# One decode block on one core: TensorE's last part placed 820 unreached instructions further on, and one load of down weights cut into 113 and 15 rows

## The chip, the cores and the metric

The kernel runs on one core of a Trainium2 chip. The metric is the time of one execution in microseconds, as the device measures it. Beside the plain timed runs there is one profiled execution, whose records the views show.

## What is computed

One decode step of a transformer block, for two batch rows and one new position: layer norm, attention over a cache of 8192 keys in 16 heads of width 256, and a bilinear gated feed-forward part, all in float32.

```python
B, Sq, D, H, Sk, Dh, F = 2, 1, 448, 16, 8192, 256, 1792
q = (layernorm(x) @ wq) as (B, H, 1, Dh)
p = softmax(einsum("bhqd,bhkd->bhqk", q, k_cache) * Dh ** -0.5)
h = x + (einsum("bhqk,bhkd->bhqd", p, v_cache) as (B, 1, H * Dh)) @ wo
n = layernorm(h)
out = h + ((n @ w_gate) * (n @ w_up)) @ w_down
```

## The kernel before

The caches make nearly all of the bytes. There are 32 pairs of head and batch row, called turns here. A turn's keys are 8192 x 256 floats, 8 MB, and lie in SBUF as 128 partitions of 64 keys each; its values lie the same way. Two key buffers take turns (`k0`, `k1`), the values have one buffer (`v`). In each turn VectorE multiplies the keys by the spread query and adds over the width (L436, L445, in a part of 16 keys and one of 48), takes the maximum (L458, L464), ScalarE makes the exponentials (L494), and TensorE mixes the values with them (L527, 32 matmuls) and gathers the four column groups (L619).

All loads but that of x are issued by SyncE, on one queue, in the order written from L261 to L292. Each load is a transfer of 128 rows, one row per partition. A load waits at SyncE until its buffer is free: keys of turn i + 1 for the maximum of turn i - 1, values of turn i for the mix of turn i - 1. After the last turn's keys and values come the weights, into buffers that the caches no longer need: the output projection `wo` and, after the last maximum, the gate weights `wg` and the up weights `wu` in three loads go to the key buffers; the down weights go to the value buffer, so they wait for the last mix, ("M", 31). They are cut into six loads by `DOWN = (4, 4, 2, 2, 1, 1)`, numbered 0 to 5; a unit is 448 columns of 128 rows (224 KB). Load 2 thus has 128 rows of 3584 bytes. TensorE waits for each of the six by its own semaphore (`wd0` to `wd5`) at the first matmul that reads it.

Each engine's instructions are recorded in a list (`Engine.do`, `roll`) and written out by `Engine.emit` (L81). A `roll` becomes a loop in the program. TensorE's list is: a short first part, a loop over the groups of the query projection (L386), a loop of 32 turns (L627, whose body also has the last turn's extra work behind branches), and the last part from L631 on: filler matmuls on data that nobody reads (`busy`, L534), the last head's output projection (L577), the second layer norm, gate and up projections (L715, L726), the product's transposes (L760), and the down projection in two forms (L779 for the chunks of loads 0 and 1, L805 for the rest), of which VectorE copies the result (L815) and SyncE stores it (L818).

`emit` also writes, at the start of each engine's list or behind the first `ahead` entries, a prefetch hint for a branch, a register `never` that holds 0, and a compare-and-branch on it. The hinted branch is a single instruction `aside` behind the engine's main part, which is never reached, since `never` is not below 0.

Of the kernel before, what the change touches and what calls it, by code (L numbers as in the profile page):

```python
# [8 lines left out]
B, D, H, SK, DH, F = 2, 448, 16, 8192, 256, 1792  # L9
EPS = 1e-5  # L10
P = 128
# [3 lines left out]
NQ = H * B  # L15
# [10 lines left out]
FH = FG[0] // 2  # L26
FF = [(n, g) for n in range(4) for g in range(4) if n < FG[g] // P]
DOWN = (4, 4, 2, 2, 1, 1)
NPART, OPEN_AFTER = 8, 9

LAYOUT = (
# [6 lines left out]
class Engine:  # L38
# [3 lines left out]
    def __init__(self, nc, engine, name, *apart):  # L42
        self.nc, self.e, self.apart = nc, engine, apart
        self.sems = [nc.alloc_semaphore(name=f"{name}{k}") for k in range(1 + len(apart))]
        self.items, self.ahead, self.gap = [], 0, None

    def sem_of(self, done):
        return self.sems[next((k + 1 for k, a in enumerate(self.apart) if done[0] in a), 0)]
# [32 lines left out]
    def emit(self, known):  # L81


        e, nc, seen = self.e, self.nc, {}
        if self.ahead is None:
            return self.emit_ops(self.items, known, seen)
        here, name = [e.engine], f"{e.engine.name}_"
        never = e.alloc_register(name + "never")
        self.emit_ops(self.items[: self.ahead], known, seen)
        hint = e.mark_branch_hint_location()  # L90
        e.reg_mov(never, 0)
        e.br_lt(never, 0, on_true=name + "aside", on_false=name + "main")
        with nc.body(name + "main", valid_engines=here):
            self.emit_ops(self.items[self.ahead : self.gap], known, seen)
            nc.br(name + "rest", engines=here)
        with nc.body(name + "aside", valid_engines=here):
            e.br_lt(never, 0, on_true=name + "aside", on_false=name + "rest").branch_hint(hint)
        nc.switch_bb(name + "rest")
        if self.gap is not None:
            self.emit_ops(self.items[self.gap :], known, seen)  # L100
# [53 lines left out]
def decode_block(nc, x, k_cache, v_cache, wq, wo, wg, wu, wd, out):  # L154
# [6 lines left out]
    def landing(name):  # L161
        return nc.alloc_semaphore(name=name)

    bank = [nc.alloc_psum_tensor(f"bank{i}", [P, 512], F32)[:] for i in range(8)]
    known = {}
    first_sem = landing("none")
    V, A, G, S, T = (
        Engine(nc, *engine)
        for engine in (
            (nc.vector, "dve"), (nc.scalar, "act", ("qsel", "qb"), ("q",)), (nc.gpsimd, "pool"),  # L170
            (nc.sync, "sp"), (nc.tensor, "pe", ("qp", "Q0"), ("heads",)),
        )
    )

    def load(line, dst, src, sem, name, *waits, n=16):
        line.do(lambda: line.e.dma_start(dst, src).then_inc(sem, 16), *waits)  # L176
        known[name] = sem, n
# [3 lines left out]
    v_flat = v_sb.rearrange("p j d -> p (j d)")  # L181
# [93 lines left out]
    at = 0  # L275
# [9 lines left out]
        load(S, wu_t[:, part], wu[:, part], landing(f"wu{k}"), ("wu", k))  # L285
    at = 0
    for k, n in enumerate(DOWN):
        load(
            S, v_flat[:, at * D : (at + n) * D], wd[:, at * D : (at + n) * D],
            landing(f"wd{k}"), ("wd", k), ("M", NQ - 1),  # L290
        )
        at += n  # L292


# [330 lines left out]
                )  # L625

    T.roll(0, NQ, 1, tensor_turn)  # L627

# [42 lines left out]
    for rows, c, to in LAYOUT:  # L673
        k = rows.stop - rows.start
# [100 lines left out]

    down_of = [k for k, n in enumerate(DOWN) for _ in range(n)]
    for k, (j, g) in enumerate(FF[:NPART]):
# [44 lines left out]
    engines = (S, A, G, V, T)  # L822
# [60 lines left out]
```

## Time and profile before

| | |
|---|---|
| plain runs, median of 3 | 1301.5 us (1301.0 to 1301.56) |
| the profiled execution | 1300.94 us |
| its span, first to last instruction | 1299.6 us |
| bytes read and written in HBM | 561.19 MB and 0.06 MB |
| VectorE busy | 1132.5 us (87%) |
| TensorE busy, matmuls | 471.1 us (36%) |
| mean granted TensorE clock | 0.64 of full speed |

The profile's page gives the time by engine and by line of the kernel; the DMA part gives packets, bytes and the share of the time of 16 DMA engines that the packets took. The chain of waits is followed back from the last instruction, at each step to what released it. The timeline lists instructions in order of time, with the idle time ahead of each and what ended it in square brackets. The windows give, for a stretch of time, its length, the busy time of the five engines (with the count of instructions), the granted TensorE clock, the mean share of the DMA engines that were busy (packets overlap, so that it can be above 1), and the GB/s moved.

### The profile page before, as it was taken

The numbers are of one execution on the slowest core, as the hardware profiler recorded it, in microseconds if no ns is written. First come the engines' busy times: TensorE is split into PE (matmuls) and PEld (weight loads), VectorE is DVE, ScalarE is ACT, GpSimd is POOL, SyncE is SP. The second block draws the span as 40 slices with busy tenths as digits, with TensorE's granted clock in tenths as the row PEclk, the third lists the DMA queues.
The fourth block names the chain that finished last, engine by engine and source line by source line (L and its number), as shares of the span: only waits on it lengthen the run. The fifth ranks groups of instructions, "written<-read, shape, count | busy, mean of one in ns | idle before, by whom it ended". The sixth has DMA issues, their size and how long they took to land.

```text
span 1299.6 us, 7381 instructions
## 1 busy us (share of the span) xinstructions
PE 471.1 (36%) x2870; PEld 149.9 (12%) x2870; DVE 1132.5 (87%) x265; ACT 83.5 (6%) x245; POOL 0.8 (0%) x8
## 2 busy tenths in 40 slices
PE   3643214334323433323334322433322343332368
PEld 0111001101001101101101101101100110100113
DVE  1999988889888889888889988889988888988861
ACT  1100000000000000000000000000000000000000
POOL 0000000000000000000000000000000000000000
PEclk9866566666566666556666656666656666655669
DMA  9999999999999999999999999999999999999998
GB/s 412 428 450 422 448 424 444 426 436 436 422 450 422 450 422 448 424 444 426 436 436 422 450 422 450 422 448 424 444 426 436 436 422 450 422 450 422 448 422 365
DMA packets 11382, 561.28 MB, mean 432 GB/s; under 512 B 1394, under 2 KB 1652, under 8 KB 2420
## 3 DMA queue, kind: packets, MB, share of 16 engines
q1 hardware_dynamic: 11376, 561.25, 99.8%
q8 instruction: 2, 0.03, 0.0%
q10 hardware_dynamic: 4, 0.00, 0.0%
HBM read 561.19 MB, written 0.06 MB: 432 GB/s over the span
## 4 chain that ended last, share of the span: by engine, by line
DMA 48%; DVE 41%; issue 8%; PE 2%; SPq 0%; DVEq 0%; ACT 0%
DMA k<-in_A_k_cache_dram 45%; DVE s L445 21%; DVE k L436 19%; DMA v<-in_wq_dram 2%; DMA v<-in_wd_dram 1%; PE bank L376 1%; PE bank L561 1%; PE bank L527 1%; DVE m L458 0%; DVE nm L464 0%; DVE rl L469 0%; SPq L176 0%; PE bank L551 0%; DVEq L149 0%; PE bank L367 0%
## 5 line engine op out<-in xcount | busy, mean ns | idle before, releaser
L436 DVE TENSOR_TENSOR k<-k,qb 128x4096 f32<-128x4096 f32 x64 | 555.3, 8676 | 122.6 <-DMA k<-in_A_k_cache_dram 98.9
L445 DVE TENSOR_REDUCE s<-k 128x16 f32<-128x4096 f32 x64 | 555.2, 8675 | 1.1
L527 PE MATMUL bank<-v,p 128*2 128x512 f32 x2048 | 289.5, 729 | 348.0 <-DMA v<-in_A_v_cache_dram 348.0
L527 PEld LDWEIGHTS bank<-v,p 128*2 128x2 f32 x2048 | 53.2, 96 | 577.2 <-DMA v<-in_A_v_cache_dram 370.7
L597 PE MATMUL bank<-nm,row 1*128 1x1 f32 x64 | 18.6, 357 | 230.9 <-DVE nm L464 230.9
L594 PE MATMUL bank<-ident,m 128*1 128x128 f32 x32 | 11.9, 372 | 179.7 <-DVE m L458 179.7
L502 ACT ACTIVATE o_sb<-bank 128x512 f32<-128x512 f32 x32 | 19.1, 597 | 625.9 <-PE bank L527 625.9
L597 PEld LDWEIGHTS bank<-nm,row 1*128 1x128 f32 x64 | 15.9, 306 | 240.3 <-DVE nm L464 240.3
L619 PE MATMUL bank<-sel,o_sb 128*128 128x1 f32 x256 | 33.7, 253 | 22.6 <-ACT o_sb L502 22.6
L367 PE MATMUL bank<-q_sel,ones 2*128 2x256 f32 x68 | 40.2, 691 | 0.0
L619 PEld LDWEIGHTS bank<-sel,o_sb 128*128 128x128 f32 x256 | 31.0, 191 | 52.3 <-ACT o_sb L502 52.3
L376 PE MATMUL bank<-v,xz 128*2 x64 | 30.5, 639 | 16.3 <-DMA v<-in_wq_dram 16.3
L492 ACT ACTIVATE nb<-bank 128x1 f32<-128x1 f32 x32 | 5.5, 171 | 427.0 <-PE bank L597 427.0
L601 PE MATMUL bank<-lsum,ones 128*128 128x1 f32 x64 | 18.7, 361 | 23.5 <-ACT p L494 23.5
L594 PEld LDWEIGHTS bank<-ident,m 128*1 128x1 f32 x32 | 2.5, 79 | 182.7 <-DVE m L458 182.7
L601 PEld LDWEIGHTS bank<-lsum,ones 128*128 128x128 f32 x64 | 16.0, 309 | 26.2 <-ACT p L494 26.2
L404 ACT ACTIVATE q_sel<-q_all,ident 2x256 f32 (+1 forms) x35 | 17.2, 492 | 0.0
L413 ACT ACTIVATE qb<-bank 128x256 f32<-128x256 f32 x34 | 13.0, 383 | 58.2 <-PE bank L367 58.2
L367 PEld LDWEIGHTS bank<-q_sel,ones 2*128 2x128 f32 x68 | 16.4, 297 | 2.2 <-issue 1.7
L494 ACT ACTIVATE p<-s,nb 128x64 f32<-128x64 f32 x32 | 11.1, 348 | 1.0
L504 ACT ACTIVATE oT<-bank,rl 128x2 f32 x32 | 8.4, 262 | 42.0 <-PE bank L619 42.0
L487 DVE COPY k<-bank 128x448 f32<-128x448 f32 x1 | 0.6, 624 | 11.6 <-PE bank L561 11.6
(89 smaller groups left out, 96.0 us busy)
## 6 DMA issues: line engine op xcount, KB each, us to landing
v<-in_wq_dram SPq DMA_DIRECT2D x1, 7168.0 KB, 19.7
k<-in_wo_dram SPq DMA_DIRECT2D x1, 7168.0 KB, 39.6
k<-in_A_k_cache_dram SPq DMA_DIRECT2D x1, 6144.0 KB, 38.1
v<-in_A_v_cache_dram SPq DMA_DIRECT2D x1, 6144.0 KB, 22.8
k<-in_wg_dram SPq DMA_DIRECT2D x1, 3136.0 KB, 27.8
k<-in_A_k_cache_dram SPq DMA_DIRECT2D x1, 2048.0 KB, 24.1
v<-in_A_v_cache_dram SPq DMA_DIRECT2D x1, 2048.0 KB, 27.3
k<-in_wu_dram SPq DMA_DIRECT2D x1, 1792.0 KB, 31.8
```

Source lines behind the costliest of these rows:

```text
L367: lambda *_: nc.tensor.matmul(qb_ps, ones[:B, :], q_sel, start=True, stop=True),
L376: lambda turn, k=k, c=c, xs=xs, base=base: nc.tensor.matmul(q_ps[k], xz[:, xs, :], wq_t[:, bass.ds(turn * QG + base, QG)], start=(c == 0), ...
L404: return nc.scalar.activation(q_sel, q_sb[:, bass.ds(at, DH)], AF.Copy, scale=ident[:B, b : b + 1])
L413: lambda *_: nc.scalar.activation(qb[i % 2], qb_ps, AF.Copy),
L436: lambda *_: nc.vector.tensor_mul(kt, kt, q[:, None, :].to_broadcast([P, hi - lo, DH])),
L445: lambda *_: nc.vector.tensor_reduce(s[:, lo:hi], kt, axis=AX.X, op=ALU.add),
L502: A.do(lambda *_: nc.scalar.activation(o_sb, o_ps, AF.Copy), ("M", i), done=("osb", i))
L527: lambda *_, t=t, g=g: nc.tensor.matmul(o_ps[g : g + 2, :], p_t[:, 2 * t : 2 * t + 2], v_sb[:, 2 * t : 2 * t + 2, :], start=(t < 4), stop= ...
L594: lambda *_: nc.tensor.transpose(mT_ps, m_t, ident), ("m", i), done=("T", i)
L597: lambda *_: nc.tensor.matmul(nb_ps, row, nm, start=True, stop=True),
L601: lambda *_: nc.tensor.matmul(l_ps, ones, lsum, start=True, stop=True),
L619: lambda *_, c=c, k=k: nc.tensor.matmul(oT_ps[:, c : c + 1], o_sb[:, (2 * k + c) * P : (2 * k + c + 1) * P], sel[:, k : k + 1], start=(k = ...
```

## The change

Two places change. First, TensorE's list gets a mark `far` behind the loop of turns. `emit` now writes the hint and the register at the start, all up to the mark, and then a compare-and-branch: if `never` is below 0 (it isn't) to a part `unused`, else to a part `far`. The hint at the start names this branch. `unused` is 1640 waits for a semaphore to be at least 0, which the built program holds as 820 instructions, and a branch; it lies between the loop and `far`, and is not reached. At `far` stand the hint, the register and the branch over `aside` that stood at the start before, and then the last part as it was. Second, load 2 of the down weights is issued as two transfers, of rows 0 to 112 and of rows 113 to 127, both to the semaphore `wd2`, whose wait asks for 32 in place of 16.

```diff
+APART, EVEN, ROWS = 820, 2, 113
...
-        self.items, self.ahead, self.gap = [], 0, None
+        self.items, self.ahead, self.gap, self.far, self.apart_by = [], 0, None, None, 0
...
         self.emit_ops(self.items[: self.ahead], known, seen)
+        at = self.ahead
+        if self.far is not None:
+            hint = e.mark_branch_hint_location()
+            e.reg_mov(never, 0)
+            self.emit_ops(self.items[at : self.far], known, seen)
+            e.br_lt(never, 0, on_true=name + "unused", on_false=name + "far").branch_hint(hint)
+            with nc.body(name + "unused", valid_engines=here):
+                for _ in range(2 * self.apart_by):
+                    e.wait_ge(self.sems[0], 0)
+                nc.br(name + "far", engines=here)
+            nc.switch_bb(name + "far")
+            at = self.far
         hint = e.mark_branch_hint_location()
         e.reg_mov(never, 0)
         e.br_lt(never, 0, on_true=name + "aside", on_false=name + "main")
         with nc.body(name + "main", valid_engines=here):
-            self.emit_ops(self.items[self.ahead : self.gap], known, seen)
+            self.emit_ops(self.items[at : self.gap], known, seen)
...
     for k, n in enumerate(DOWN):
-        load(
-            S, v_flat[:, at * D : (at + n) * D], wd[:, at * D : (at + n) * D],
-            landing(f"wd{k}"), ("wd", k), ("M", NQ - 1),
-        )
+        sem, parts = landing(f"wd{k}"), [slice(0, P)]
+        if k == EVEN:
+            parts = [slice(0, ROWS), slice(ROWS, P)]
+        for rows in parts:
+            load(
+                S, v_flat[rows, at * D : (at + n) * D], wd[rows, at * D : (at + n) * D],
+                sem, ("wd", k), ("M", NQ - 1), n=16 * len(parts),
+            )
         at += n
...
     T.roll(0, NQ, 1, tensor_turn)
+    T.far, T.apart_by = len(T.items), APART
```

On TensorE, where the loop of turns ends, the order was the following (`bank` is PSUM, `o_sb` the mixed values, `oT` the heads' results, `sel`, `heads` and `ident` constants or earlier results; the waits are for ScalarE's semaphore `act0`):

```order
L619 MATMUL bank<-sel,o_sb 128x1 [waits act0]
L619 MATMUL bank<-sel,o_sb 128x1 x3
L115 REGISTER_ALU
L115 COMPARE_AND_BRANCH
L539 MATMUL bank<-k,sel 2x256 x4
L581 MATMUL bank<-k,oT 2x256 [waits act0]
```

It now is this, with the line numbers of the changed file (L639 was L619, L559 was L539, L601 was L581; the 820 waits of `unused` are not listed, and lie ahead of the branch of L103):

```order
L639 MATMUL bank<-sel,o_sb 128x1 [waits act0]
L639 MATMUL bank<-sel,o_sb 128x1 x3
L131 REGISTER_ALU
L131 COMPARE_AND_BRANCH
L99 COMPARE_AND_BRANCH
L103 UNCONDITIONAL_BRANCH [waits pe0]
L106 BRANCH_PREFETCH_HINT
L108 COMPARE_AND_BRANCH
L559 MATMUL bank<-k,sel 2x256 x4
L601 MATMUL bank<-k,oT 2x256 [waits act0]
```

Behind the loop's own branch (L131) stands the new one (L99), which goes past L103 to L106; the matmuls and their waits are as before.

On SyncE, from the load of the up weights to the output, the order was the following (`k` and `v` are the buffers; the numbers are rows by floats):

```order
L176 DMA k<-in_wu_dram 128x896
L176 DMA v<-in_wd_dram 128x1792 [waits pe0]
L176 DMA v<-in_wd_dram 128x1792
L176 DMA v<-in_wd_dram 128x896 x2
L176 DMA v<-in_wd_dram 128x448 x2
```

It now is:

```order
L192 DMA k<-in_wu_dram 128x896
L192 DMA v<-in_wd_dram 128x1792 [waits pe0]
L192 DMA v<-in_wd_dram 128x1792
L192 DMA v<-in_wd_dram 113x896
L192 DMA v<-in_wd_dram 15x896
L192 DMA v<-in_wd_dram 128x896
L192 DMA v<-in_wd_dram 128x448 x2
```

One issue has become two, and loads 3 to 5 stand one issue later; nothing else on this queue is moved.

## The prediction

> **What bounds the kernel now.** I read the page's header and queue table first, then the end of the chain of waits, then the windows of the last microseconds. The page:
>
> ```profile
> span 1299.6 us, 7381 instructions
> ...
> DMA packets 11382, 561.28 MB, mean 432 GB/s; under 512 B 1394, under 2 KB 1652, under 8 KB 2420
> ...
> q1 hardware_dynamic: 11376, 561.25, 99.8%
> q8 instruction: 2, 0.03, 0.0%
> q10 hardware_dynamic: 4, 0.00, 0.0%
> ```
>
> SyncE's queue q1 keeps the 16 DMA engines busy for 99.8% of the span, so bytes per engine set the time. One engine moves 561.25 MB / (0.998 x 16 x 1299.6 us) = 27,046 bytes per us. The packet count also says how a transfer is dealt. The code issues 79 transfers of 128 rows on q1 (78 loads, one output), and 79 x (128 + 16) = 11,376: each row is a packet and each transfer has 16 more. These are the small ones: 79 x 16, 2 on q10 and the output's 128 rows of 448 bytes make the 1394 under 512 bytes. The last steps of the chain, with start, duration and what ran:
>
> ```profile
> 1278.38 0.42 SPq L176
> 1278.85 0.43 SPq L176
> 1279.31 17.89 DMA v<-in_wd_dram
> 1297.24 0.44 PE bank L805 x8
> 1297.71 0.27 DVE k L815
> ```
>
> The last load of down weights is issued by 1279.31 and lands about 1297.2, 17.89 us later, though it has 0.2 MB: it stands behind what is queued. From 1297.24 to the end of the span are 2.36 us. Windows (length, busy time of each engine, granted clock, mean DMA share, GB/s):
>
> ```profile
> 1290.00:1292.00 2.00, 2.00 (x16) 0.51 (x14) 0.74 (x2) 0.00 (x0) 0.00 (x0) 1.00 1.00 421
> ...
> 1295.00:1295.50 0.50, 0.35 (x16) 0.38 (x16) 0.50 (x1) 0.00 (x0) 0.00 (x0) 1.00 0.94 362
> 1295.50:1296.00 0.50, 0.50 (x20) 0.16 (x8) 0.06 (x1) 0.00 (x0) 0.00 (x0) 1.00 0.25 93
> 1296.00:1296.50 0.50, 0.36 (x18) 0.35 (x16) 0.00 (x0) 0.00 (x0) 0.00 (x0) 1.00 0.13 50
> 1296.50:1297.00 0.50, 0.50 (x20) 0.16 (x9) 0.00 (x0) 0.00 (x0) 0.00 (x0) 1.00 0.09 36
> 1297.00:1297.50 0.50, 0.34 (x12) 0.16 (x8) 0.00 (x0) 0.00 (x0) 0.00 (x0) 1.00 0.00 0
> ```
>
> The share falls from 0.94 to 0.25, then to 0.13 and 0.09: 0.13 x 16 is two engines. So some 14 engines are done near 1295.6 and about two work on until 1297.2. The kernel ends with its slowest DMA engine, some 1.6 us behind most. TensorE's timeline says how its last waits follow the loads:
>
> ```profile
> 1290.14 0.20 PEld L726 LDWEIGHTS bank<-k,xr 128*64 128x64 f32 x4 [0.84 <-DMA k<-in_wu_dram]
> ...
> 1293.93 0.93 PE L779 MATMUL bank<-v,k 128*2 128x448 f32 x8 [0.23 <-DMA v<-in_wd_dram]
> ...
> 1295.15 0.59 PE L805 MATMUL bank<-v,k 128*32 128x112 f32 x16 [0.29 <-DMA v<-in_wd_dram]
> ...
> 1296.15 0.93 PE L805 MATMUL bank<-v,k 128*32 128x112 f32 x24
> ...
> 1297.24 0.40 PE L805 MATMUL bank<-v,k 128*32 128x112 f32 x8 [0.16 <-DMA v<-in_wd_dram]
> ```
>
> From wu2 on TensorE waits for a load at nearly every group, but only 0.16 to 0.84 us each.
>
> **The load in two parts.** Load 2 of the down weights (448 KB, 128 rows of 3584 bytes, 8 rows per engine) becomes one of 113 and one of 15 rows. The bytes stay; what counts is which engine gets them. One more issue costs SyncE about 0.43 us (the chain's last SPq row), and it moves loads 3 to 5 back by that at the issue, about 17 us ahead of their landing; the output's issue waits for VectorE anyway. So that is nothing. Nothing waits earlier than before either: TensorE's wait for load 2 now asks for both parts. The deal is the whole cost. The trace shows one transfer with other than 128 rows, the two rows of x on ScalarE's queue, in the first 4 us:
>
> ```profile
> DMA packets 20, 0.92 MB, mean 230 GB/s; under 512 B 2, under 2 KB 4, under 8 KB 4
> ...
> q1 hardware_dynamic: 16, 0.92, 70.2%
> q10 hardware_dynamic: 4, 0.00, 0.6%
> ```
>
> Of q10's four packets two are rows (1792 bytes) and two are small: a transfer closes with one small packet for each engine that took part, two for two rows and 16 for 128. In both cases every engine had an equal share, 1 row or 8. By that, 15 rows go to 15 engines. But 113 is prime: equal shares exist only as 113 engines or as one, so one engine gets all 113. Unequal shares (8 rows on fourteen engines, 1 on a fifteenth, none on the last) are the other way; no row excludes them. I take equal shares, since nothing else occurs in the trace.
>
> [...]
>
> The sum. The one engine gets 113 rows and one of the 15, where it had 8: 106 more rows of 3584 bytes. At 27,046 bytes per us that is 106 x 0.1325 = 14.05 us. From the timeline: loads 4 and 5 (28,672 bytes per engine together) part the waits at 1296.15 and 1297.24, 1.09 us, so 0.136 us per 3584 bytes and 14.4 us in all. I take 14.2. Its queue then ends at 1295.6 + 14.2 = 1309.8, if it is one of the fourteen; loads 3 to 5 need their share of this engine too and land behind. The end moves from 1297.24 by 12.6 us. If it is one of the late two, by 14.2 us. Fourteen of sixteen: I take 12.6. The other engines have 7 or 8 rows less, and nothing follows from that: a load counts as landed with its last engine.
>
> One thing comes on top. TensorE now waits over 10 us with nothing to do, and an earlier such pause shows what follows:
>
> ```profile
> 1250.00:1252.00 2.00, 0.00 (x0) 0.00 (x0) 2.00 (x1) 0.00 (x0) 0.00 (x0) 0.93 1.06 459
> 1252.00:1254.00 2.00, 0.00 (x0) 0.00 (x0) 1.97 (x2) 0.00 (x0) 0.00 (x0) 0.50 0.86 373
> ...
> 1260.00:1262.00 2.00, 2.00 (x16) 0.45 (x12) 0.00 (x0) 0.00 (x0) 0.00 (x0) 0.50 0.91 393
> ```
>
> The granted clock was 0.50 after it and still so 6 us into work. The last group after the last landing took 0.44 us at clock 1.00; at half clock 0.88. Bounds 0 and +0.5; I take +0.3, since only part of a group is clock.
>
> **The part further on.** TensorE gets a compare-and-branch over 820 instructions, named by the hint at the program's start; the hint, register and branch that stood at the start come again behind it, at the head of the last part. Around this place:
>
> ```profile
> 1277.63 1.05 PE L619 MATMUL bank<-sel,o_sb 128*128 128x1 f32 x8
> 1278.61 0.61 PE L539 MATMUL bank<-k,sel 128*2 128x256 f32 x8
> 1279.19 0.81 PE L581 MATMUL bank<-k,oT 128*2 128x256 f32 x6
> ```
>
> The loop's closing branch already stands between the first two rows and shows no gap, so two more branches are bounded by nothing and some tenths. If the code at the target must be fetched first, there is a stall. Fetches show as q8, two in the run; this is the one of 1282 to 1285:
>
> ```profile
> q8 instruction: 1, 0.02, 2.0%
> ```
>
> 2.0% of 16 engines' 3 us is 0.96 us for one. It may stand behind one data packet, for the gate weights 25,088 bytes / 27,046 = 0.93 us. So 0 to 1.9 us per fetch; I take nothing on the path, because in my forecast TensorE is more than 10 us early for load 2, and 0.84 us early already for wu2. A fetch also takes its 0.96 us from one DMA engine; that counts only if it is the loaded one, 1 in 16, and is left out.
>
> 12.6 + 0.3 = 12.9 us. The profiled execution took 1300.94 us, span 1299.6 and 1.34 around it; the median 1301.5 is 0.56 above. On the median: 1301.5 + 12.9 = 1314.4 us. The forecast's own range: 14.05 - 1.64 = 12.4 without the clock gives 1313.9, a late engine with 14.4 + 0.5 gives 1316.4.
>
> **Rivals.** First, the rows are dealt unequally: 8 to each of fourteen engines, 1 to the fifteenth, and the 15 rows one each to fifteen. Then two engines have 8 and 6 rows less (1.06 and 0.80 us), the others one more (0.13 us). If the two are the late ones, the last landing comes up to 1.06 us sooner; TensorE's waits of 0.16 to 0.29 us let it follow by about 0.7: 1300.8 us. If they are others, 1301.6. For it: two late engines are there to be relieved, by nearly these amounts. Against it: no unequal share in the trace. This is not slower, where I forecast slower; it decides as soon as 113 rows run on 14 engines or more.
>
> Second, the far part is not there when TensorE jumps: with the unequal deal, and three fetches of 1.9 us one after the other as an upper end (the last part is longer than one packet), 5.7, less the 0.84 and 0.29 that TensorE waits for loads today, is 4.6: 1306.1 us. It decides above some 1.1 us of stall. Against it: the hint at the program's start names this branch. [...]
>
> **How the numbers follow.** Forecast 0.57, first rival 0.36, second 0.05, and 0.02 for a gain of over 0.2% (2.6 us; what a measurement here can tell from no change), for which the late engines' 1.6 us are too little. Slower 0.57 + 0.05 = 0.62, same 0.36, faster 0.02. Leaving out the first rival would leave out more than 2 in 10, so the range reaches from that rival's 1300.8 to the forecast's 1316.4, with 0.3 on each side for the scatter of the runs (1301.0 to 1301.56): 1300.5 to 1316.7. Where the forecast holds, 1313.9 to 1316.4.
>
> **What would show it.** Right: a wait of over 10 us for in_wd ahead of the first L805 group (L826 in the new file), a DMA share near 1/16 for some 13 us, and q1 still at 11,376 packets (113 + 1 and 15 + 15 replace 128 + 16). Wrong: 11,390 packets or more (15 or 16 closing packets for 113 rows), no long wait, and a span within 2 us of 1299.6. A gap ahead of L539's group behind the loop would be the fetch.

## The result, and the profile after

The changed kernel takes 1315.32 us (median of 5 runs, 1314.98 to 1315.46) against 1301.28 us of the kernel before beside it (1300.84 to 1301.56): a ratio of 1.0108, with a 95% interval of 1.0093 to 1.0123. That is 14.04 us slower; 12.9 were forecast. The profiled execution took 1315.46 us, 1.36 more than its span.

The page of the changed kernel, header and queues:

```profile
span 1314.1 us, 7385 instructions
...
q1 hardware_dynamic: 11376, 561.25, 98.7%
q8 instruction: 2, 0.03, 0.0%
q10 hardware_dynamic: 4, 0.00, 0.0%
```

The bytes and the packets of q1 are the same as before, 11,376: 113 rows with one closing packet and 15 rows with 15 have replaced 128 rows with 16. Only the share of busy engines is less, 98.7%, in a longer span. Its windows from 1290 us on (length, busy time of PE, PEld, DVE, ACT and POOL with counts, granted clock, DMA share, GB/s):

```profile
1290.00:1292.00 2.00, 2.00 (x16) 0.50 (x14) 0.76 (x2) 0.00 (x0) 0.00 (x0) 1.00 1.01 423
...
1294.00:1295.00 1.00, 0.91 (x8) 0.08 (x8) 0.03 (x1) 0.00 (x0) 0.00 (x0) 1.00 0.06 25
...
1296.00:1300.00 4.00, 0.00 (x0) 0.00 (x0) 0.00 (x0) 0.00 (x0) 0.00 (x0) 0.65 0.71 224
...
1301.00:1309.00 8.00, 0.00 (x0) 0.00 (x0) 0.00 (x0) 0.00 (x0) 0.00 (x0) 0.50 0.06 26
...
1310.50:1311.00 0.50, 0.50 (x17) 0.50 (x13) 0.00 (x0) 0.00 (x0) 0.00 (x0) 0.50 0.07 29
1311.00:1311.50 0.50, 0.50 (x19) 0.48 (x15) 0.00 (x0) 0.00 (x0) 0.00 (x0) 0.50 0.00 0
```

From 1294 to 1295 us the share is 0.06, which is one engine of 16, moving 25 GB/s. From 1296 to 1300 the others come back for the 15 rows and loads 3 to 5, and from 1301 to 1311 one engine is left at 26 GB/s. TensorE and VectorE have nothing to do in that time, and the granted clock falls to 0.50. TensorE's and SyncE's lines of the timeline show who waited:

```profile
1276.95 20.66 SPq L192 DMA_DIRECT2D v<-in_wd_dram  x7
...
1293.97 0.94 PE L800 MATMUL bank<-v,k 128*2 128x448 f32 x8 [0.29 <-DMA v<-in_wd_dram]
...
1309.32 0.98 PE L826 MATMUL bank<-v,k 128*32 128x112 f32 x16 [14.41 <-DMA v<-in_wd_dram]
...
1310.04 0.63 PE L816 MATMUL bank<-k,rep 128*32 128x112 f32 x8
...
1310.41 1.75 PE L826 MATMUL bank<-v,k 128*32 128x112 f32 x32
1312.22 0.27 DVE L836 COPY k<-bank 128x112 f32<-128x112 f32 x1 [16.62 <-PE bank L826]
```

The wait of 0.29 us ahead of the first down-projection group that reads load 2 has become 14.41 us. The same 16 matmuls took 0.59 us before and take 0.98 at half clock. New, too, is SyncE's row: its seven issues take 20.66 us, where six took 3.27. The end of the chain of waits:

```profile
1277.97 0.30 SPq L192
1278.28 0.06 issue
1278.34 30.85 DMA v<-in_wd_dram
1309.19 0.14 issue
1309.32 0.98 PE bank L826 x16
1310.30 0.37 PE bank L816 x8
1310.67 1.53 PE bank L826 x32
1312.20 0.02 issue
1312.22 0.27 DVE k L836
```

From the landing of load 2 on, no load is on the chain: TensorE works through its remaining 56 matmuls without a wait (2.88 us), and loads 3 to 5 land meanwhile. Before, the last group still waited for load 5.

The 113 rows are issued in 0.30 us at 1277.97. The next issue, of the 15 rows, begins at 1278.34 and holds SyncE, as this row of SyncE's timeline says, for 17.73 us:

```profile
1278.34 17.73 SPq L192 DMA_DIRECT2D v<-in_wd_dram  x1
```

So loads 3 to 5 are issued only after 1296. That gives a second reading of the 14 us, which had to be told from the first: one engine's bytes, or SyncE's hold-up.

### The profile page after: what moved, and what is told of

The parts are those of the page before. It is cut to its first block, busy times and chain, and to the rows that moved or that the text cites. A ratio compares the mean times of both kernels' runs of the same rounds, so it can differ in the third digit from the quotient of the medians.

```text
span 1314.1 us, 7385 instructions
## 1 busy us (share of the span) xinstructions
PE 471.1 (36%) x2870; PEld 150.9 (11%) x2870; DVE 1132.6 (86%) x265; ACT 83.5 (6%) x245; POOL 0.8 (0%) x8
## 3 DMA queue, kind: packets, MB, share of 16 engines
q1 hardware_dynamic: 11376, 561.25, 98.7%
## 4 chain that ended last, share of the span: by engine, by line
DMA 75%; PE 25%; issue 0%; SPq 0%; DVE 0%
DMA v<-in_A_v_cache_dram 71%; PE bank L547 22%; DMA v<-in_wd_dram 2%; PE bank L396 2%; DMA v<-in_wq_dram 1%; PE bank L826 0%; SPq L192 0%; PE bank L387 0%; PE bank L816 0%; DVE k L836 0%
## 5 line engine op out<-in xcount | busy, mean ns | idle before, releaser
L639 PE MATMUL bank<-sel,o_sb 128*128 128x1 f32 x256 | 33.7, 253 | 22.6 <-ACT o_sb L522 22.6
L639 PEld LDWEIGHTS bank<-sel,o_sb 128*128 128x128 f32 x256 | 31.0, 191 | 52.3 <-ACT o_sb L522 52.3
```

Source lines behind the costliest of these rows:

```text
L639: lambda *_, c=c, k=k: nc.tensor.matmul(oT_ps[:, c : c + 1], o_sb[:, (2 * k + c) * P : (2 * k + c + 1) * P], sel[:, k : k + 1], start=(k = ...
```

## The experiments

Three theories: the **one-engine theory** (113 rows have no equal shares but one, so one engine moves them all, and its bytes are the price), the **blocked-issue theory** (the price is that loads 3 to 5 are issued 17.7 us late), and the **far-part theory** (the jump over 820 instructions and its fetches). Each experiment is the changed kernel with the edit shown; all but two, the far part alone and the one that joins 126 and 2 rows with the far part, also leave out the line that sets `T.far`, so that TensorE's last part stands where it was. "Before" is the kernel before, run beside them.

**The two halves of the change.** The far part alone:

```diff
-APART, EVEN, ROWS = 820, 2, 113
+APART, EVEN, ROWS = 820, None, 113
```

> The far part alone, the load whole. One-engine theory (all of the cost is one DMA engine that has 113 rows): as before, 1301.3 us within 0.5, no wait of over 1 us for the down weights. Far-part theory (the jump or its fetches cost): several us above before. Blocked-issue theory (the cost is SyncE, which was held up 17.7 us at the issues of load 2): as before, too, with seven issues in about 3 us.

Measured: 1301.19 us (11 runs) against 1301.25, ratio 0.9999 (0.9990 to 1.0008). TensorE's timeline around the jump:

```profile
1277.57 1.05 PE L639 MATMUL bank<-sel,o_sb 128*128 128x1 f32 x8
1278.56 0.61 PE L559 MATMUL bank<-k,sel 128*2 128x256 f32 x8
1279.14 0.81 PE L601 MATMUL bank<-k,oT 128*2 128x256 f32 x6
```

The jump lies between the first two rows, which follow each other as before: no gap. The far-part theory falls, and nothing of the 14 us is this edit's. The split alone:

```diff
-    T.far, T.apart_by = len(T.items), APART
```

> The load as 113 and 15 rows alone, the last part where it was. One-engine theory: the full cost, 1315.3 us within 0.7, q1 at 11,376 packets. Blocked-issue theory: the same. Far-part theory: near 1301.

Measured: 1315.56 us (1315.28 to 1315.68) against 1301.25, ratio 1.0110 (1.0095 to 1.0126): the whole cost, at 11,376 packets.

**Bytes on one engine, or a hold-up at SyncE.** Other rows, then another place, then narrower rows:

```diff
-APART, EVEN, ROWS = 820, 2, 113
+APART, EVEN, ROWS = 820, 2, 122
```

> The load as 122 and 6 rows, the last part where it was. One-engine theory with equal shares: 122 is 2 x 61, so two engines have 61 rows and one more each, 54 above the 8 of before, 54 x 0.1365 us = 7.4 us; the changed kernel's 14 us for 106 rows scales to 7.1: 1308.5 us, 1307.5 to 1309.5. If an unequal deal or a fixed price for an odd count were behind it: near 1301 or again 1315. Blocked-issue theory: no size given, as long as SyncE's longest issue.

Measured: 1308.78 us (1308.41 to 1308.9), ratio 1.0057 (1.0041 to 1.0072), 7.5 us above before. The windows of this run while the wait lasts:

```profile
1298.00:1300.00 2.00, 0.00 (x0) 0.00 (x0) 0.00 (x0) 0.00 (x0) 0.00 (x0) 0.87 0.12 50
1300.00:1302.00 2.00, 0.00 (x0) 0.00 (x0) 0.00 (x0) 0.00 (x0) 0.00 (x0) 0.50 0.13 54
```

A share of 0.12 to 0.13 and 50 to 54 GB/s are two engines, as 122 = 2 x 61 says. In the next run the 113 rows are the last transfer on the queue:

```diff
         if k == EVEN:
-            parts = [slice(0, ROWS), slice(ROWS, P)]
+            parts = [slice(ROWS, P)]
+            long = at, n, sem
...
         at += n
+    at, n, sem = long
+    load(
+        S, v_flat[:ROWS, at * D : (at + n) * D], wd[:ROWS, at * D : (at + n) * D],
+        sem, ("wd", EVEN), ("M", NQ - 1), n=32,
+    )
```

> The 15 rows where load 2 stands, the 113 rows as the last transfer on the queue, behind load 5, the last part where it was. Nothing is issued behind the long transfer, so loads 3 to 5 aren't held up. One-engine theory: the one engine has the same rows, its end stays at about 1311.4 us, and TensorE now has all of the L805 work behind it (2.9 us from the first to VectorE's copy in the changed kernel, about 1.5 more than there): 1316.5 us, 1315 to 1318. Blocked-issue theory: the hold-up costs nothing now, so most of the 14 us goes: below 1306.

Measured: 1317.2 us (1316.8 to 1317.32), ratio 1.0121 (1.0106 to 1.0137). SyncE's seven issues and the windows of this run:

```profile
1276.91 3.12 SPq L192 DMA_DIRECT2D v<-in_wd_dram  x7
```

```profile
1300.00:1308.00 8.00, 0.00 (x0) 0.00 (x0) 0.00 (x0) 0.00 (x0) 0.00 (x0) 0.50 0.06 26
...
1310.00:1311.00 1.00, 0.00 (x0) 0.00 (x0) 0.00 (x0) 0.00 (x0) 0.00 (x0) 0.50 0.04 18
1311.00:1312.00 1.00, 0.83 (x20) 0.86 (x24) 0.00 (x0) 0.00 (x0) 0.00 (x0) 0.50 0.00 0
```

The hold-up is gone, 3.12 us for all issues, and the time is not better but 1.6 us worse (1317.2 against the 1315.56 of the split alone): the one engine is busy until about 1311 as before, and more of TensorE's work is left behind it. The blocked-issue theory falls. Then load 4, of 1792-byte rows, is split in place of load 2:

```diff
-APART, EVEN, ROWS = 820, 2, 113
+APART, EVEN, ROWS = 820, 4, 113
```

> Load 4 (rows of 1792 bytes) as 113 and 15 rows, load 2 whole, the last part where it was. One-engine theory, by bytes: 106 rows more of 1792 bytes on one engine, half of 14 us: 1308.3 us, 1307 to 1309. If each row costs the same whatever its size: again about 1315.

Measured: 1307.66 us (1307.55 to 1307.8), ratio 1.0048 (1.0032 to 1.0064), 6.3 us above before: nearly half of the 14.3 us that the split of load 2 alone cost. The price goes by bytes, not by rows. The length of the hold-up doesn't set the price either: SyncE's seven issues lasted 14.57 us with 122 and 6 rows, at 7.5 us above before, 20.56 with the split of load 2 alone, at 14.3 us, and 3.12 with the 113 rows last, at 15.95 us.

**Splits that leave no engine with much.** These ask whether the rival's even deal could be had in another way.

```diff
-APART, EVEN, ROWS = 820, 2, 113
+APART, EVEN, ROWS = 820, 2, 126
```

> The load as 126 and 2 rows, the last part where it was. Equal shares: 126 is 14 x 9, so fourteen engines have 9 rows, two of them one more, and two engines have none, 8 less (1.09 us). No long wait: 1301.3 us within 0.3 if these two are not the late ones, 1300.4 to 1300.8 if they are. If it is the second transfer or the odd size as such that costs: several us more.

Measured: 1302.83 us (11 runs, 1302.3 to 1303.63) against 1301.32, ratio 1.0011 (1.0002 to 1.0021). The same split together with the far part:

> 126 and 2 rows with the last part further on. As with 126 and 2 rows alone, within 0.4 us; if the far part moves the instruction fetch to one of the relieved engines, up to 0.8 us better than before, 1300.5 us.

Measured: 1302.92 us, ratio 1.0012 (1.0003 to 1.0022). With `ROWS` 112:

> The load as 112 and 16 rows, the last part where it was: both run on 16 engines, 7 and 1 rows each. Equal shares: the bytes on every engine are as before, so 1301.3 us within 0.3; the second transfer's issue and closing packets cost nothing. If two transfers as such cost: more, by the size of that.

Measured: 1302.91 us, ratio 1.0014 (1.0005 to 1.0023). With `ROWS` 120:

> The load as 120 and 8 rows, the last part where it was. Equal shares: 120 is 15 x 8, so fifteen engines have 8 rows and eight of them one more, the sixteenth has none (1.09 us less). 1301.3 us within 0.4: one late engine at most is relieved, and the other still ends last.

Measured: 1303.06 us, ratio 1.0015 (1.0006 to 1.0024). There is no long wait, as the one-engine theory says (TensorE's longest for the down weights is 1.33 us with 126 and 2 rows and 1.53 with 112 and 16), but each of the four costs 1.5 to 1.7 us, and that was foreseen by none; 112 and 16 rows put the same number of rows on every engine as 128 do. With 126 and 2 rows a part of it may be TensorE's clock, which was 0.50 of full speed from 1297 to 1299; with 112 and 16 rows it was 1.00. The windows of the run with 112 and 16 rows, while load 2 lands:

```profile
1292.00:1293.00 1.00, 1.00 (x16) 0.49 (x18) 0.80 (x3) 0.00 (x0) 0.00 (x0) 1.00 0.98 401
1293.00:1294.00 1.00, 0.73 (x8) 0.00 (x0) 0.00 (x1) 0.00 (x0) 0.00 (x0) 1.00 1.12 294
1294.00:1295.00 1.00, 0.00 (x0) 0.00 (x0) 0.00 (x0) 0.00 (x0) 0.00 (x0) 1.00 0.96 280
```

In the kernel before the same three windows have:

```profile
1292.00:1293.00 1.00, 1.00 (x16) 0.48 (x18) 0.78 (x3) 0.00 (x0) 0.00 (x0) 1.00 1.00 409
1293.00:1294.00 1.00, 0.77 (x12) 0.07 (x8) 0.00 (x0) 0.00 (x0) 0.00 (x0) 1.00 1.01 412
1294.00:1295.00 1.00, 0.86 (x8) 0.04 (x8) 0.07 (x1) 0.00 (x0) 0.00 (x0) 1.00 1.01 396
```

The engines are as busy (0.96 to 1.12 against 1.01), but move 280 to 294 GB/s in place of 396 to 412: the packets take longer. Either the deal of rows does it, or the second transfer. Three runs tell these apart. Load 2 as two transfers of all 128 rows, half of the columns each:

```diff
-        if k == EVEN:
-            parts = [slice(0, ROWS), slice(ROWS, P)]
-        for rows in parts:
+        for q in (0, 1) if k == EVEN else (None,):
+            lo, hi = (at, at + n) if q is None else (at + q, at + q + 1)
             load(
-                S, v_flat[rows, at * D : (at + n) * D], wd[rows, at * D : (at + n) * D],
+                S, v_flat[:, lo * D : hi * D], wd[:, lo * D : hi * D],
...
```

> Load 2 as two transfers of 128 rows and 448 columns each, the last part where it was. The earlier cuts into two parts of rows on 14 to 16 engines each cost about 1.5 us, which no theory so far had foreseen. Row-deal theory (with fewer than 128 rows the rows go to the engines in another way, and the engines' packets hold each other up): nothing here, 1301.3 us within 0.3. Second-transfer theory (one more issue and 16 more closing packets cost): again about 1302.9.

Measured: 1301.24 us against 1301.32, ratio 0.9999 (0.9990 to 1.0009). The second transfer cost nothing here. Load 0, with twice the bytes, as 64 and 64 rows (`EVEN, ROWS = 0, 64`):

> Load 0 (896 KB, rows of 7168 bytes) as 64 and 64 rows, load 2 whole, the last part where it was. Row-deal theory: slower, and by more than the 1.5 us of the cuts of load 2 (448 KB), since twice the bytes are concerned: 1303 to 1305 us, with a low rate at a full DMA share while load 0 lands. Second-transfer theory: about 1302.9, the same as with load 2.

Measured: 1304.76 us, ratio 1.0028 (1.0017 to 1.0038). Load 0 as 112 and 16 rows (`EVEN, ROWS = 0, 112`):

> Load 0 as 112 and 16 rows, load 2 whole, the last part where it was. Row-deal theory: twice the 1.5 us that the same cut of load 2 cost, 1304.3 us, 1303.5 to 1305. Second-transfer theory: the same 1302.9 as there.

Measured: 1304.42 us, ratio 1.0024 (1.0013 to 1.0034), 3.1 us above before; the same cut of half the bytes cost 1.6. So it is the cut by rows and not the second transfer, and it goes by bytes. Why the packets of such a cut took longer, the row-deal theory's second half, is not shown. The windows of the run with 64 and 64 rows, while load 0 lands:

```profile
1289.00:1290.00 1.00, 0.75 (x10) 0.16 (x8) 0.00 (x0) 0.00 (x0) 0.00 (x0) 1.00 1.14 233
1290.00:1291.00 1.00, 0.80 (x8) 0.00 (x0) 0.00 (x0) 0.00 (x0) 0.00 (x0) 1.00 1.09 219
```

The rate is about half of the 430 and 423 GB/s that the kernel before has in these two windows.

## Why the prediction was right, step by step

**The deal.** Right, and now shown. The forecast rested on equal shares, argued from 2 and 128 rows alone. The packets of q1 bear it out for every split in the table, if a transfer closes with one packet per engine, as the 2 small packets of the two rows of x and the 16 of each load of 128 rows say:

| rows of load | engines by equal shares | q1 packets expected | q1 packets on the page |
|---|---|---|---|
| 113 and 15 | 1 and 15 | 11,376 | 11,376 |
| 122 and 6 | 2 and 6 | 11,368 | 11,368 |
| 126 and 2 | 14 and 2 | 11,376 | 11,376 |
| 120 and 8 | 15 and 8 | 11,383 | 11,383 |
| 112 and 16 | 16 and 16 | 11,392 | 11,392 |

An unequal deal of 113 rows over 15 engines would give 11,390. The count gives only the sum of the engines of both transfers, 16 for 113 and 15 rows; that the 113 rows have one engine is shown by the share of 0.06.

**The size.** The loaded engine's queue was put to end at 1309.8 us. Windows of 0.1 us, two of the kernel before and two of the changed one, show where the last row starts:

```profile
1296.80:1296.90 0.10, 0.10 (x8) 0.04 (x5) 0.00 (x0) 0.00 (x0) 0.00 (x0) 1.00 0.05 18
1296.90:1297.00 0.10, 0.10 (x8) 0.00 (x0) 0.00 (x0) 0.00 (x0) 0.00 (x0) 1.00 0.01 0
...
1310.90:1311.00 0.10, 0.10 (x9) 0.10 (x5) 0.00 (x0) 0.00 (x0) 0.00 (x0) 0.50 0.09 36
1311.00:1311.10 0.10, 0.10 (x11) 0.10 (x7) 0.00 (x0) 0.00 (x0) 0.00 (x0) 0.50 0.01 0
```

The end came at 1311.1, 1.3 us later than forecast, and moved by 14.1 us, where 12.6 were forecast. Of this difference 0.3 is a slip: the forecast measured its move from 1297.24, where TensorE's last group starts, and the DMA engines were done at 1296.9.

The loaded engine was taken for one of the fourteen that end first, and it was one. In the changed kernel, from 1292.6 to 1293.5, three engines are busy:

```profile
1292.60:1293.50 0.90, 0.90 (x16) 0.17 (x8) 0.35 (x2) 0.00 (x0) 0.00 (x0) 1.00 0.17 72
```

```profile
DMA packets 12, 0.06 MB, mean 72 GB/s; under 512 B 0, under 2 KB 0, under 8 KB 12
```

Twelve packets at 72 GB/s for 0.9 us are six rows of load 1 (7168 bytes) and six of load 2 (3584 bytes). Two engines are late with load 1, then, and the loaded one is already at load 2.

The 1.3 us come from three sizes. First, the price of a row: from 1301 to 1309 the lone engine moved 59 rows (61 packets, two of them closing ones), 0.136 us each:

```profile
DMA packets 61, 0.21 MB, mean 26 GB/s; under 512 B 2, under 2 KB 2, under 8 KB 61
```

That is 14.4 us for 106 rows, where 14.2 was taken. (The forecast's second reading had this price, although its row at 1296.15 shows no wait.) Second, the fourteen were put to end at 1295.6, but three engines were still busy from 1295.9 to 1296.0 (share 0.18), so one of the fourteen ended up to 0.4 us later; whether it was the loaded one, no run shows. Third, nothing was put down for other loads that run beside the lone engine. Of its 122 rows of 3584 bytes (113, one of the 15, and 8 of load 3), 67 start after 1300.7, as the packets from 1300.7 to 1311.1 say (88, of which 21 are under 2 KB):

```profile
DMA packets 88, 0.27 MB, mean 26 GB/s; under 512 B 5, under 2 KB 21, under 8 KB 88
```

The 55 rows before took from 1292.6 to 1300.7, 8.1 us, where 0.136 us each make 7.5. In part of that time, from 1296 to 1300, a share of 0.71 moved 224 GB/s; at the 423 GB/s of a share of 1.01 it would be 297. Packets took longer there, and why is open.

So the measured time lies inside the range partly by luck. With an early engine the forecast's own bounds end at 1301.5 + 14.4 - 1.64 + 0.5 = 1314.8 us; the 1316.4 stood for a late engine. The engine was an early one, and 1315.3 was reached by delays that the forecast didn't have.

**The clock.** Taken at +0.3 of at most 0.5, it was right in size and wrong in path. From the first group that reads load 2 to VectorE's copy were 2.56 us before (1295.15 to 1297.71) and are 2.90 now (1309.32 to 1312.22): +0.34. The forecast had TensorE wait for the last landing and run one group behind it at half clock. In fact TensorE waited for load 2 alone, and all 56 matmuls left were behind that wait at a clock of 0.50; the last landing was no longer waited for. The start of that first group moved by 14.17 us, and 14.17 + 0.34 = 14.5, the difference of the spans.

**SyncE's extra issue.** This step was wrong: it was taken as 0.43 us, and the issue of 15 rows lasted 17.73. It cost nothing because loads 3 to 5 ended behind the one engine anyway, as the run with the 113 rows last shows: no hold-up there, and the DMA work again ends near 1311.

**The far part.** Right: nothing (0.9999). The second rival's stall did not occur. Its 5.7 us stood for three fetches in a row, on the estimate that the last part is longer than one packet; no run shows its length or more than one fetch for it. The run with the far part alone has two q8 packets in all (0.03 MB), as the kernel before has. The one in the last part is still there, but earlier: in the run with the far part alone it lies between 1281 and 1283, where the kernel before has none until 1282.9, 3.0% of 16 engines' 2 us, 0.96 us:

```profile
q8 instruction: 1, 0.02, 3.0%
```

**The first rival** fell with its deal. Its price, a gain of 0.7 us if the two relieved engines were the late ones, was never met as such, since no run dealt rows unequally. The nearest, 126 and 2 rows, takes 7 or 8 rows from each of two engines and was 0.11% slower; whether these two were the late ones, the runs don't show, but the cost of a cut by rows, which the rival left out, outweighed what there was to gain.

## What to carry to other kernels

Before a transfer is cut by rows, look at what divides the number of rows: 113 rows, a prime number, were all on one of 16 DMA engines here, at 26 GB/s in place of 423, and 122, 2 x 61, on two, at 50 to 54. The packet count on a profile's page agreed with how many engines the transfers had together, one small packet for each (11,376 for 113 and 15 rows, 11,368 for 122 and 6, 11,392 for 112 and 16), without any timing. And where a load must be cut, try it by columns first, with all 128 rows kept: that was free here (0.9999), while cuts by rows were not, even with equal numbers of rows on all engines (1.0014 with 112 and 16 rows).

## What the runs showed of the hardware that was not expected

In these runs cuts by rows lowered the rate at a full DMA share (0.96 to 1.14): 280 to 294 GB/s with 112 and 16 rows, 219 to 233 with 64 and 64, against 396 to 430 for 128 rows in the same stretch. The cost grew with the bytes (1.6 and 3.1 us for 448 and 896 KB as 112 and 16 rows). No run here shows why.

A transfer of 113 rows on one engine was issued in 0.30 us, but the issue behind it held SyncE for 17.73 us; with 122 and 6 rows the seven issues took 14.57 us in all, and with the 113 rows last 3.12. What SyncE waits for there, these runs do not tell.
